# Linear attention and two gated layers on one core: GpSimd's jobs cut up, a new order, another check, and loads on two queues

## The chip, the cores and the metric

One Trainium2 chip, of which one core is used. The core has TensorE (matmuls, PE in the profile), VectorE (DVE), ScalarE (ACT), GpSimd (POOL), and SyncE (SP), which here only issues transfers. The metric is the device time of one execution in microseconds; the median of the runs counts.

## What is computed

A linear attention with decay runs over 4 batches x 8 heads, 768 positions, head width 48. Its result, 3072 tokens of width 384, goes through a gated layer of inner width 1536, then through an RMS norm and a second such layer.

```python
state = 0                                   # per batch and head, 48 x 48
for t in range(768):
    y[t] = r[t] @ (state + (u * k[t]) v[t]^T)
    state = w * state + k[t] v[t]^T
x = y as (3072, 384)
x = (silu(x @ w_gate) * (x @ w_val)) @ w_out            # first layer
xn = x / sqrt(mean(x * x) + 1e-6) * rms_g
out = (silu(xn @ w_gate2) * (xn @ w_val2)) @ w_out2     # second layer
```

The weights of both layers and the queries, keys and values come in as they lie in HBM; weights are 64-bit floats, which the kernel takes apart by their bits.

## The kernel before

The attention is done in 32 units: a batch, a half of the sequence (384 positions) and two heads. Units 0 to 3 (`Unit`) work in chunks of 128, units 4 to 15 (`FullUnit`) in chunks of 64, and the rest (`SplitUnit`) with every operand split into two 16-bit parts. Four units make one block of 384 tokens; there are eight blocks. A block passes each layer in 12 steps, one for each 128 of the inner width. A step has three parts of nine matmuls on TensorE: `step_g` (the gate, `pg`), `step_v` (the value, `pv`), `step_o` (the output, which sums over the 12 steps in three accumulators `po0` to `po2`, one for 128 tokens each). Between them ScalarE computes the silu (`step_s`, tile `sl`), VectorE the product (`step_m`, `sl` again), ScalarE the upper part `hh` (`step_hh`), and GpSimd the lower part `hl` (`step_hl`); `step_o` needs both parts.

The blocks run in the order `ORD`: three blocks of the first layer, then the layers by turns. After a first-layer block its accumulators are copied out (`evacuate`), squared and summed (`squares`, ScalarE), the inverse root and its relatives are formed on three columns (`inverse_rms`, GpSimd: four `ms`, the power `ri`, then `rr` and `iratio`), the tokens scaled, turned and stored. Later they come back (`load_x2`), and `ratio_x2` on GpSimd multiplies them for the second layer's value path.

Each weight tile (one for a step and layer, 24 in all) is decoded: ScalarE takes two passes over it for the check of its range (`w_abs`, `w_check`), VectorE three integer steps (`w_bits`) and one for the lower part (`w_lo`), ScalarE one for the upper (`w_hi`).

The order on every engine is laid out when the program is built. `Plan.add` takes a job with its engine, an expected duration, the jobs it comes after, and a latency; `Plan.run` ranks each job by the longest expected path behind it and fills the engines in expected time, the highest rank first. What a job issues stays together in its engine's queue, and each queue runs in order. A job `D` issues transfers on SP.

The first units: `load` brings keys (`kts`) and queries (`rts`) in four transfers each, all on SP, keys and queries by turns; the values come by GpSimd's own queue. `turn` (VectorE) turns them, `decay_keys` and `grow` (GpSimd, VectorE for the first keys) multiply with the tables G and F, `products` (GpSimd) forms `kr`; `states` (VectorE) carries the state over the chunks, `hand_on` and `states2` (ScalarE) write the carry for the next half and the scaled states for the matmuls. `split_tables` (GpSimd) prepares tables that the units from the fifth on need.

At the end a flag is formed: `check_range` brings all bounds together, `check_last` adds the last block, whose sums of squares come from ScalarE's pass over the accumulators `po`. If the flag is set, a general path runs instead; with these inputs it is not.

Of the kernel before, what the change touches and what calls it, by code (L numbers as in the profile page):

```python
# [18 lines left out]
P = 128  # L19
# [120 lines left out]
def fast_path(ctx, tc, r, k, v, w, u, wg1, wv1, wo1, wg2, wv2, wo2, rms_g, out):  # L140
# [56 lines left out]

    iratio = c_tile([P, NBLK * NG], "iratio")
# [135 lines left out]
    class Unit:  # L334
# [18 lines left out]
        def load(self, which):  # L353
            self.load_rows((self.kts, self.rts)[which], (k, r)[which])
# [127 lines left out]
    class SplitUnit(Unit):  # L482
# [237 lines left out]
    def split_tables():  # L720
# [14 lines left out]
        g.tensor_scalar(out=w_carry, in0=p2[:, 1], scalar1=2.0**AB, scalar2=None, op0=ALU.mult)  # L735
# [128 lines left out]
    def on_act(layer, blk):  # L864

        return () if (layer, blk) == (1, NBLK - 1) else (1,) if layer else (0, 1)
# [15 lines left out]
    def squares(layer, blk):  # L882
        for g in range(NG):
            sq = ev.tile([P, DM], F32, tag="sq", name="sq")
            col = (layer * NBLK + blk) * NG + g
            if (layer, blk) == (1, NBLK - 1):
                nc.scalar.activation(out=sq, in_=acc[layer, blk][g], func=AF.Square, accum_out=ssall[:, col : col + 1],
                                     scale=iratio[:, blk * NG + g : blk * NG + g + 1])
            else:
                nc.scalar.activation(out=sq, in_=post["xo", layer, blk][:, g], func=AF.Square, accum_out=ssall[:, col : col + 1])  # L890

    def inverse_rms(blk):

        g, ms = nc.gpsimd, ev.tile([P, 4, NG], F32, tag="ms", name="ms")
        ss = ssall[:, blk * NG : (blk + 1) * NG]
        for i in range(4):
            g.tensor_scalar(out=ms[:, i], in0=ss, scalar1=1.0 / DM, scalar2=1e-30 if i % 2 else 1e-6, op0=ALU.mult, op1=ALU.add)
        pw_ = post["ri"] = ev.tile([P, 4, NG], F32, tag="ri", name="ri")
        g.tensor_tensor(out=pw_, in0=ms, in1=powers, op=ALU.pow)
# [39 lines left out]
    def ratio_x2(xt, rrow):  # L939
# [84 lines left out]

    def check_last():
# [53 lines left out]
    add("rmsg", "D", 0.5, [("lr", HP - 1)], setup_loads2)  # L1079
    add("bonus", "D", 0.95, [("lr", HP - 1)], setup_loads3)  # L1080
# [4 lines left out]
    add("ws0", "G", 0.4, ["c1"], lambda: nc.gpsimd.memset(wscan, 0.0))  # L1085
# [393 lines left out]
```

## Time and profile before

| | |
|---|---|
| median of 3 runs | 1028.3 us (1027.5 to 1030.15) |
| profiled execution | 1029.09 us, span 1027.4 us |
| mean granted clock | 0.976 |
| TensorE busy | 980.6 us (95%) |
| VectorE, ScalarE, GpSimd busy | 523.4, 519.5, 436.8 us |
| ScalarE in the last four of 40 slices, tenths | 2, 3, 2, 2 |
| one part of a step (nine matmuls) at full clock | 1.46 us |

The profile cuts the span into 40 slices of 25.7 us and gives each engine's busy share in tenths. A clock of 1.00 is TensorE's upper level, 2.4 GHz; 0.50 is its lower level, 1.2 GHz; a mean between them says how a stretch was divided. In lists of instructions a bracket gives the idle time of the engine ahead of the instruction, and who ended it.

### The profile page before, as it was taken

How to read it: one execution, taken by the hardware profiler on the slowest of the kernel's cores; microseconds unless marked ns; L12 is line 12 of the kernel's file. 1: busy time of each engine (PE TensorE's matmuls, PEld its weight loads, DVE VectorE, ACT ScalarE, POOL GpSimd, SP SyncE). 2: the span in 40 equal slices, each digit the busy share in tenths (PEclk: the TensorE clock that was granted, in tenths of full speed). 3: DMA queues.
4: the chain of work that ended last, by engine and by line, in shares of the span. 5: the costliest groups of instructions: out<-in, count | busy, mean ns of one | idle time of the engine just before them, and what ended most of it. 6: DMA issues, size and time to landing. Idle time of an engine off the chain costs nothing.

```text
span 1027.4 us, 19923 instructions
## 1 busy us (share of the span) xinstructions
PE 980.6 (95%) x7903; PEld 612.8 (60%) x7903; DVE 523.4 (51%) x817; ACT 519.5 (51%) x1121; POOL 436.8 (43%) x489
## 2 busy tenths in 40 slices
PE   6887898989999999999999999999999999999996
PEld 3655665646666666666666666666666666666663
DVE  6889997997634434474443534464332412131211
ACT  1987755865644745474455635465453524342322
POOL 9255474444353435544455335544343223321121
PEclk7889998999999999999999999999999999999998
DMA  7988765647441312331122311321010100200000
GB/s 179 226 217 208 219 185 121 169 125 125 108 47 35 84 41 46 58 94 42 33 34 51 83 41 41 64 60 41 2 24 2 54 1 3 53 24 1 24 1 27
DMA packets 152741, 76.87 MB, mean 75 GB/s; under 512 B 115648, under 2 KB 141248, under 8 KB 152640
## 3 DMA queue, kind: packets, MB, share of 16 engines
q1 hardware_dynamic: 152256, 74.93, 30.7%
q8 instruction: 64, 1.05, 0.5%
q0 software_dynamic: 384, 0.59, 0.3%
q14 instruction: 37, 0.30, 0.1%
HBM read 66.03 MB, written 9.45 MB: 73 GB/s over the span
## 4 chain that ended last, share of the span: by engine, by line
PE 70%; DVE 7%; POOL 6%; ACT 6%; issue 4%; DMA 4%; SPq 2%; DVEq 0%; POOLq 0%; ACTq 0%
PE pv L852 22%; PE pg L852 22%; PE po L862 22%; PE py L566 3%; ACT sb L630 2%; POOL hl L992 2%; POOL ap L524 2%; DMA raw<-in_moe_w_out_dram 1%; PE pd L577 1%; DVE st L614 1%; SPq L361 1%; DVE fi L819 1%; DVE fi L821 1%; ACT hh L988 1%; DVE w L842 1%
## 5 line engine op out<-in xcount | busy, mean ns | idle before, releaser
L852 PEld LDWEIGHTS <-w 128*128 128x128 f16 x3456 | 336.4, 99 | 237.4 <-issue 22.3
L992 POOL TENSOR_TENSOR hl<-sl,hh 128x384 f16<-128x384 f32 x191 | 188.2, 986 | 472.4 <-ACT hh L988 465.9
L862 PE MATMUL po<-w,hh 128*128 128x384 f16 x1152 | 282.8, 328 | 1.3 <-ACT xo L878 1.3
L988 ACT ACTIVATE hh<-sl 128x384 f16<-128x384 f32 x192 | 100.0, 521 | 339.9 <-DVE sl L982 194.8
L862 PE MATMUL po<-w,hl 128*128 128x384 f16 x576 | 189.0, 328 | 7.8 <-POOL hl L992 7.7
L982 DVE SCALAR_TENSOR_TENSOR sl<-sl,pv 128x384 f32<-128x384 f32 x96 | 53.1, 554 | 236.0 <-PE pv L852 203.0
L852 PE MATMUL pg<-xh,w 128*128 128x384 f16 x576 | 159.0, 331 | 12.1 <-DVE sl L984 9.6
L852 PE MATMUL pv<-xh,w 128*128 128x384 f16 x576 | 159.4, 332 | 0.0
L862 PEld LDWEIGHTS <-hh 128*128 128x128 f16 x1152 | 111.9, 98 | 74.4 <-issue 2.5
L852 PE MATMUL pv<-x2v,w 128*128 128x384 f16 x864 | 156.2, 326 | 0.0
L852 PE MATMUL pg<-x2g,w 128*128 128x384 f16 x864 | 156.1, 326 | 0.0
L984 DVE TENSOR_TENSOR sl<-sl,pv 128x384 f32<-128x384 f32 x96 | 52.7, 550 | 121.4 <-PE pv L852 117.3
L974 ACT ACTIVATE sl<-pg 128x384 f32<-128x384 f32 x192 | 93.3, 486 | 28.9 <-PE pg L852 27.9
L852 PE MATMUL pg<-xl,w 128*128 128x384 f16 x288 | 95.4, 331 | 1.3 <-DVE xl L479 1.3
L852 PE MATMUL pv<-xl,w 128*128 128x384 f16 x288 | 95.6, 332 | 0.0
L862 PEld LDWEIGHTS <-hl 128*128 128x128 f16 x576 | 56.6, 98 | 47.4 <-POOL hl L992 9.6
L614 DVE TENSOR_TENSOR_SCAN st<-wscan,pd 128x288 f32<-128x288 f32 x28 | 21.0, 750 | 45.6 <-ACT pd L609 26.1
L566 PE MATMUL py<-rp,sb 128*128 128x64 f16 (+1 forms) x400 | 39.3, 212 | 0.4 <-ACT sb L688 0.4
L842 DVE SCALAR_TENSOR_TENSOR w<-fi,w 128x1152 f16<-128x1152 f32 (+1 forms) x30 | 36.6, 1229 | 1.3 <-ACT w L838 1.3
L838 ACT ACTIVATE w<-fi 128x1152 f16<-128x1152 f32 (+1 forms) x30 | 28.8, 963 | 13.0 <-DVE fi L821 12.9
L475 ACT ACTIVATE xh<-py 96x384 f16<-96x384 f32 (+1 forms) x42 | 20.2, 482 | 27.9 <-PE py L566 27.6
L819 DVE SCALAR_TENSOR_TENSOR fi<-raw,fi 128x1152 int32<-128x1152 int32 x21 | 32.4, 1544 | 0.4
(209 smaller groups left out, 1190.2 us busy)
## 6 DMA issues: line engine op xcount, KB each, us to landing
raw<-in_moe_w_out_dram SPq DMA_DIRECT2D x21, 384.0 KB, 5.4
kts<-in_k_dram SPq DMA_DIRECT2D x112, 70.0 KB, 2.8
rts<-in_r_dram SPq DMA_DIRECT2D x112, 70.0 KB, 2.0
xs_d<-tt SPq DMA_DIRECT2D x32, 144.0 KB, 3.8
xt<-xs_d SPq DMA_DIRECT2D x32, 144.0 KB, 3.1
nk<-in_k_dram SPq DMA_DIRECT2D x56, 72.0 KB, 2.7
nr<-in_r_dram SPq DMA_DIRECT2D x56, 72.0 KB, 2.5
out_dram<-xo SPq DMA_DIRECT2D x7, 576.0 KB, 2.9
```

The source lines that it names most:

```text
L566: nc.tensor.matmul(out, a, x, start=i == 0, stop=i == len(pairs) - 1)
L614: nc.vector.tensor_tensor_scan(st, wscan, self.pd, 0.0, ALU.mult, ALU.add)
L819: vec.scalar_tensor_tensor(out=fis[q], in0=high, scalar=-0x40000000, in1=fis[q], op0=ALU.bitwise_and, op1=ALU.bitwise_or)
L838: nc.scalar.activation(out=w_parts(q)[0], in_=fis[q].bitcast(F32), func=AF.Copy, scale=2.0**WS)
L842: nc.vector.scalar_tensor_tensor(out=lo, in0=fis.pop(q).bitcast(F32), scalar=2.0**WS, in1=hi, op0=ALU.mult, op1=ALU.subtract)
L852: nc.tensor.matmul(pt, a[:, kt, :], x[:, kt, :], start=i == 0, stop=i == last)
L862: nc.tensor.matmul(po[g], a[:, sl], x, start=f == 0 and i == 0, stop=f == NF - 1 and i == 2)
L974: nc.scalar.activation(out=sl, in_=job[t]["g"], func=AF.Silu, scale=2.0 ** -(WS + (X2S if J[0] else X1S)))
L982: nc.vector.scalar_tensor_tensor(out=sl, in0=sl, scalar=2.0 ** (H2S - WS - V2S), in1=job[t]["v"], op0=ALU.mult, op1=ALU.mult)
L984: nc.vector.tensor_mul(sl, sl, job[t]["v"])
L988: nc.scalar.activation(out=job[t]["h"][0], in_=job[t]["sl"], func=AF.Copy)
L992: (nc.vector if t == 2 * NT - 1 else nc.gpsimd).tensor_sub(hl, job[t]["sl"], hh)
```

## The change

It has four parts.

- GpSimd: `inverse_rms` becomes three jobs, `ratio_x2` three (one for each third of the width), and the two multiplications of the attention's `products` two.
- The order: most durations and some latencies given to `Plan.add` are others; `split_tables` is placed behind the products of the fourth unit; the transfers of `rmsg` and `u` come behind the last first keys.
- ScalarE's `hand_on` and `states2` of units 0 to 3 go to VectorE, as does the table `w_carry`. The queries of those units are loaded by ScalarE's queue.
- The last block: each step's `hh` is squared and summed on ScalarE (`step_q`), `check_most` and `check_last` look at those sums, and there is no pass over the accumulators; the second of the three accumulators is copied out by ScalarE instead of VectorE.

```diff
+    hsum = c_tile([P, NF], "hsum")
...
-        def load_rows(self, t, src):
+        def load_rows(self, t, src, eng=nc.sync):
...
-                    nc.sync.dma_start(out=t[q : q + 32, 0:RUN],
-                                      in_=bass.AP(src.tensor, self.off(j) + 16 * h, [[NP2 * D, 32], [1, RUN]]))
+                    eng.dma_start(out=t[q : q + 32, 0:RUN],
+                                  in_=bass.AP(src.tensor, self.off(j) + 16 * h, [[NP2 * D, 32], [1, RUN]]))
...
         def hand_on(self):
 
-            nc.scalar.activation(out=carry[self.hp], in_=self.st[:, NC], func=AF.Copy, scale=w_carry[:, self.hp : self.hp + 1])
+            nc.vector.tensor_scalar(out=carry[self.hp], in0=self.st[:, NC], scalar1=w_carry[:, self.hp : self.hp + 1], scalar2=None,
+                                    op0=ALU.mult)
 
         def states2(self):
             for j in range(2):
                 q = slice(64 * j, 64 * j + 64)
-                nc.scalar.activation(out=sbd[self.par][q, :, D * j : D * j + D], in_=self.st[q, 0:NC], func=AF.Copy,
-                                     scale=w128(self.hp)[q])
+                nc.vector.tensor_scalar(out=sbd[self.par][q, :, D * j : D * j + D], in0=self.st[q, 0:NC], scalar1=w128(self.hp)[q],
+                                        scalar2=None, op0=ALU.mult)
...
         def products(self):
-            rk = self.rk = b_tile([P, N2, D], "rk")
-            nc.gpsimd.tensor_mul(rk, self.nr, self.nk)
+            self.rk = b_tile([P, N2, D], "rk")
+            nc.gpsimd.tensor_mul(self.rk, self.nr, self.nk)
+
+        def products2(self):
+            rk = self.rk
             nc.gpsimd.tensor_mul(rk, rk, u2[:, self.hp].unsqueeze(1).to_broadcast([P, N2, D]))
...
-        return () if (layer, blk) == (1, NBLK - 1) else (1,) if layer else (0, 1)
+        return (1,) if layer else (0, 1)
...
+    def inverse_rms2():
+        post["ri"] = ev.tile([P, 4, NG], F32, tag="ri", name="ri")
+        nc.gpsimd.tensor_tensor(out=post["ri"], in0=post.pop("ms"), in1=powers, op=ALU.pow)
...
-        xv = xi.tile([P, KT, TB], F32, tag="tt", name="xv")
-        nc.gpsimd.tensor_mul(xv, xt, rrow.unsqueeze(1).to_broadcast([P, KT, TB]))
-        return xv
+    def ratio_x2(j, kt):
+        xt, rrow = post["xt", j]
+        if not kt:
+            post["xv", j] = xi.tile([P, KT, TB], F32, tag="tt", name="xv")
+        nc.gpsimd.tensor_mul(post["xv", j][:, kt], xt[:, kt], rrow)
...
+    def step_q(t):
+
+        jk = ev.tile([P, TB], BF16, tag="sq", name="jq")
+        f = t - 2 * NT + NF
+        nc.scalar.activation(out=jk, in_=job[t]["h"][0], func=AF.Square, accum_out=hsum[:, f : f + 1])
...
-        ok = ev.tile([P, NG], F32, tag="ok3", name="ok3")
-        nc.vector.tensor_scalar(out=ok, in0=ssall[:, -NG:], scalar1=FINITE, scalar2=None, op0=ALU.is_le)
+        ok = ev.tile([P, 1], F32, tag="ok4", name="ok4")
+        nc.vector.tensor_scalar(out=ok, in0=hsum[:, NF - 1 :], scalar1=FINITE, scalar2=None, op0=ALU.is_le)
...
-    add("rmsg", "D", 0.5, [("lr", HP - 1)], setup_loads2)
-    add("bonus", "D", 0.95, [("lr", HP - 1)], setup_loads3)
+    add("rmsg", "D", 0.5, [("lk", HP - 1)], setup_loads2)
+    add("bonus", "D", 0.95, [("lk", HP - 1)], setup_loads3)
...
-        add(("lk", n), "D", 1.8, [("lr", i - 1)] if i else ["wu"], lambda un=un: (un.stage(un.n), un.load(0)))
-        add(("lr", n), "D", 1.8, [("lk", n)], lambda un=un: un.load(1))
+        add(("lk", n), "D", 1.8, [("at", n)] + ([("lk", i - 1)] if i else ["wu"]), lambda un=un: un.load(0, nc.sync))
+        add(("lr", n), "A", 1.8, [("at", n)] + ([("lr", i - 1)] if i else ["table"]), lambda un=un: un.load(1, nc.scalar), lat=4.0)
...
-        add(("cy", n), "A", 0.25, [("st", n), "tables2"], lambda un=un: un.hand_on())
-        add(("sbd", n), "A", 0.82, [("st", n), "c1"] + prior("y", 2), lambda un=un: un.states2())
+        add(("cy", n), "V", 0.13, [("st", n), "w_carry"], lambda un=un: un.hand_on())
+        add(("sbd", n), "V", 0.4, [("st", n), "c1"] + prior("y", 2), lambda un=un: un.states2())
...
-    add("tables2", "G", 4.5, ["tables", "c1"], split_tables)
+    add("w_carry", "V", 0.1, ["tables"], carry_scale)
+    add("tables2", "G", 4.5, ["tables", "c1", ("rk", HP - 1)], split_tables)
...
-        job_("rk", "G", 1.9, [("nk", n), ("nr", n), "u2", "split"] + p("sums"), lambda un=un: un.products())
-        job_("sums", "V", 0.44, [("rk", n)] + p("eg"), lambda un=un: un.sums())
+        job_("rk", "G", 1.05, [("nk", n), ("nr", n), "split"] + p("sums"), lambda un=un: un.products())
+        job_("rku", "G", 1.05, [("rk", n), "u2"], lambda un=un: un.products2())
+        job_("sums", "V", 0.44, [("rku", n)] + p("eg"), lambda un=un: un.sums())
...
-        add(("abs",) + q, "A", 0.19 + 0.96 * scale, [("w",) + q] + step("chk", prev) + (held(q) if q[0] else []), lambda: w_abs(q))
-        add(("chk",) + q, "A", 0.28 + 0.96 * scale, [("abs",) + q, "c1"], lambda: w_check(q))
+        add(("w",) + q, "D", wcost, ready, (lambda: w_load(*q)) if len(q) == 2 else (lambda: w_load2(q[1], q[2])), lat=5.0 if q[0] else 8.0)
+        add(("abs",) + q, "A", 0.24 + 1.2 * scale, [("w",) + q] + step("chk", prev) + (held(q) if q[0] else []), lambda: w_abs(q))
+        add(("chk",) + q, "A", 0.24 + 1.2 * scale, [("abs",) + q, "c1"], lambda: w_check(q))
...
-            add(("ri", blk), "G", 2.5, [("sq",) + J] + back("put") + back("sc"), lambda blk=blk: inverse_rms(blk))
-            add(("sc", blk), "A", 1.6, [("ri", blk)], lambda blk=blk: normalize(blk))
+            add(("ms", blk), "G", 1.5, [("sq",) + J] + back("ri"), lambda blk=blk: inverse_rms(blk))
+            add(("ri", blk), "G", 2.4, [("ms", blk)] + back("sc") + back("rr"), lambda: inverse_rms2())
+            add(("rr", blk), "G", 1.1, [("ri", blk)] + back("put"), lambda blk=blk: inverse_rms3(blk))
+            add(("sc", blk), "A", 1.75, [("ri", blk)], lambda blk=blk: normalize(blk))
...
-    add("bad", "V", 0.5, ["check", ("sq",) + ORD[-1]] + [("e",) + ORD[-1] + (g,) for g in range(NG)],
+    add("most", "V", 0.4, ["check", ("hq", 2 * NT - 2)], check_most)
+    add("bad", "V", 0.5, ["most", ("hq", 2 * NT - 1), ("o", 2 * NT - 1)] + [("e",) + ORD[-1] + (0,)],
         lambda: post.__setitem__("bad", check_last()))
```

## Rows read from the trace of the kernel before

**Rows 1.** The page's slices: TensorE's busy share in tenths, 40 slices.

```profile
PE   6887898989999999999999999999999999999996
```

**Rows 2.** Stretches: length, busy us of each engine, clock, DMA share, GB/s; last, the first 300 us.

```profile
10.00:20.00 10.00, 3.27 (x18) 3.04 (x18) 9.50 (x19) 0.00 (x0) 9.53 (x27) 0.64 0.72 174
20.00:30.00 10.00, 9.41 (x70) 7.20 (x70) 4.44 (x14) 6.37 (x19) 6.01 (x7) 0.67 0.99 240
...
sum 300.00, PE 264.57 PEld 171.93 DVE 247.67 ACT 193.64 POOL 158.17; mean PE 8.82 PEld 5.73 DVE 8.26 ACT 6.45 POOL 5.27
```

**Rows 3.** Stretches around and behind the long waits, same columns (PE, PEld, DVE, ACT, POOL).

```profile
156.00:163.00 7.00, 5.87 (x28) 2.88 (x30) 2.12 (x5) 4.03 (x7) 4.83 (x8) 0.52 0.63 95
...
150.00:230.00 80.00, 72.39 (x576) 45.15 (x574) 73.04 (x89) 56.21 (x106) 39.36 (x42) 0.94 0.54 138
230.00:300.00 70.00, 70.00 (x548) 45.09 (x546) 44.62 (x77) 38.44 (x93) 31.82 (x37) 0.99 0.54 99
```

**Rows 4.** Waits of TensorE over the whole span: us in total, times, longest.

```profile
PE pg L852 <- DVE sl L984: 9.6, 6, 3.8
PE att L420 <- POOL first L388: 7.8, 1, 7.8
PE po L862 <- POOL hl L992: 7.7, 4, 3.6
```

**Rows 5.** Instructions in order of time at the start: start us, us, engine, line.

```profile
2.25 1.72 SPq L361 DMA_DIRECT2D first<-in_k_dram  x4
...
9.38 1.52 DVE L377 STREAM_TRANSPOSE first<-first 128x384 f32<-128x384 f32 x2
...
10.19 0.31 POOL L725 TENSOR_SCALAR xs<-E 128x32 f32<-128x32 f32 x1
...
10.95 0.38 DVE L306 TENSOR_TENSOR F<-E,pw 128x128 f32<-128x128 f32 x1
...
15.68 1.00 POOL L388 TENSOR_TENSOR first<-first,F 128x384 f32<-128x384 f32 x1
...
17.64 0.42 SPq L770 DMA_DIRECT2D raw<-in_moe_w_gate_dram  x1
...
26.07 0.76 DVE L817 TENSOR_SCALAR fi<-raw 128x1152 int32<-128x1152 int32 x1 [1.99 <-DMA raw<-in_moe_w_out_dram]
```

**Rows 6.** Instructions in order of time behind the first blocks' last steps.

```profile
149.23 0.51 ACT L988 ACTIVATE hh<-sl 128x384 f16<-128x384 f32 x1
149.41 2.90 POOL L897 TENSOR_SCALAR ms<-ssall 128x3 f32<-128x3 f32 x4 [1.51 <-ACT sq L890]
...
152.40 2.92 POOL L899 TENSOR_TENSOR ri<-ms,powers 128x12 f32<-128x12 f32 x1
...
156.16 1.79 POOL L992 TENSOR_TENSOR hl<-sl,hh 128x384 f16<-128x384 f32 x2
...
157.13 0.50 PE L862 MATMUL po<-w,hl 128*128 128x384 f16 x1 [3.56 <-POOL hl L992]
...
228.57 0.50 PE L862 MATMUL po<-w,hl 128*128 128x384 f16 x1 [2.32 <-POOL hl L992]
```

**Rows 7.** Instructions in order of time: a step of the last block.

```profile
985.02 0.91 POOL L992 TENSOR_TENSOR hl<-sl,hh 128x384 f16<-128x384 f32 x1 [3.47 <-ACT hh L988]
...
989.64 0.33 PE L862 MATMUL po<-w,hl 128*128 128x384 f16 x1
```

**Rows 8.** Groups by line and shape: busy us, mean ns of one; idle time ahead.

```profile
L451 ACT ACTIVATE sbd<-st,p 64x144 f32<-64x144 f32 x8 | 3.2, 405 | 0.1
...
L302 DVE TENSOR_SCALAR iE<-iE,zm 128x64 f32<-128x64 f32 x1 | 0.3, 253 | 0.1
```

**Rows 9.** Instructions in order of time at the end.

```profile
1016.68 0.62 DVE L880 TENSOR_SCALAR xo<-po,iratio 128x384 f32<-128x384 f32 x1 [0.43 <-PE po L862]
...
1018.74 1.32 DVE L880 TENSOR_SCALAR xo<-po,iratio 128x384 f32<-128x384 f32 x2 [1.45 <-ACT sq L887]
...
1020.52 0.15 DVE L1033 TENSOR_SCALAR bad<-pc 1x1 int32<-1x1 f32 x1 [0.38 <-PE pc L1031]
```

More of the change, by code (lines that the diff above doesn't have):

```diff
@@ L351, in stage, with load @@
             self.turned = [t[:, n + i * TB : n + (i + 1) * TB].rearrange("p (c t) -> p c t", c=NC) for i in range(2)]
[L353 to L356 removed]
+        def load(self, which, eng):
+            self.load_rows((self.kts, self.rts)[which], (k, r)[which], eng)
+        def load_rows(self, t, src, eng=nc.sync):
             for j in range(2):
@@ L734, in split_tables, with carry_scale @@
             g.tensor_copy(m2[q], mask[q, q])
-        g.tensor_scalar(out=w_carry, in0=p2[:, 1], scalar1=2.0**AB, scalar2=None, op0=ALU.mult)
+    def carry_scale():
+        nc.vector.tensor_scalar(out=w_carry, in0=p2[:, 1], scalar1=2.0**AB, scalar2=None, op0=ALU.mult)
     def split_decay():
@@ L885, in squares @@
             col = (layer * NBLK + blk) * NG + g
[L886 to L890, printed above, removed]
+            nc.scalar.activation(out=sq, in_=post["xo", layer, blk][:, g], func=AF.Square, accum_out=ssall[:, col : col + 1])
     def inverse_rms(blk):
         g, ms = nc.gpsimd, ev.tile([P, 4, NG], F32, tag="ms", name="ms")
+        post["ms"] = ms
         ss = ssall[:, blk * NG : (blk + 1) * NG]
@@ L1023, in check_range, with check_most @@
         nc.vector.tensor_mul(post["m2"], m1[:, 0:1], m1[:, 1:2])
+    def check_most():
+        ok, m1 = ev.tile([P, NF - 1], F32, tag="ok3", name="ok3"), ev.tile([P, 1], F32, tag="m3", name="m3")
+        nc.vector.tensor_scalar(out=ok, in0=hsum[:, : NF - 1], scalar1=FINITE, scalar2=None, op0=ALU.is_le)
+        nc.vector.tensor_reduce(out=m1, in_=ok, axis=AX.X, op=ALU.min)
+        nc.vector.tensor_mul(post["m2"], post["m2"], m1)
     def check_last():
-        ok = ev.tile([P, NG], F32, tag="ok3", name="ok3")
-        nc.vector.tensor_scalar(out=ok, in0=ssall[:, -NG:], scalar1=FINITE, scalar2=None, op0=ALU.is_le)
+        ok = ev.tile([P, 1], F32, tag="ok4", name="ok4")
+        nc.vector.tensor_scalar(out=ok, in0=hsum[:, NF - 1 :], scalar1=FINITE, scalar2=None, op0=ALU.is_le)
         pc = ps.tile([P, 1], F32, tag="att0", name="pc")
-        for i in range(NG + 1):
-            nc.tensor.matmul(pc[0:1], ok[:, i - 1 : i] if i else post["m2"], ones, start=i == 0, stop=i == NG)
+        for i, x in enumerate((post["m2"], ok)):
+            nc.tensor.matmul(pc[0:1], x, ones, start=i == 0, stop=i == 1)
         bad = ev.tile([1, 1], I32, tag="bad", name="bad")
-        nc.vector.tensor_scalar(out=bad, in0=pc[0:1], scalar1=(NG + 1) * P - 0.5, scalar2=None, op0=ALU.is_lt)
+        nc.vector.tensor_scalar(out=bad, in0=pc[0:1], scalar1=2 * P - 0.5, scalar2=None, op0=ALU.is_lt)
         return bad
@@ L1179, in fast_path @@
         for w_, users in (("k", ("rk", "ex", "sq")), ("r", ("rk", "sq")), ("v", ("v1", "sq"))):
-            job_("n" + w_, "D", 0.9, [("lk", n)] + [x for us in users for x in p(us, 2)] + ([("y", NU2 - 1)] if w_ == "v" and n < NU2 + 2 else []),
+            job_("n" + w_, "D", 1.3, [("lk", n)] + [x for us in users for x in p(us, 2)] + ([("y", NU2 - 1)] if w_ == "v" and n < NU2 + 2 else []),
                  lambda un=un, w_=w_: un.load_natural(w_))
@@ L1250, in fast_path @@
         if len(q) == 3:
-            w_jobs(q, 1 / 3, 1.4, [("lo",) + seq[i - 2]], ahead)
+            w_jobs(q, 1 / 3, 2.0, [("lo",) + seq[i - 2]], ahead)
             continue
-        ready = [("lr", HP - 1)] + ([("w", 0, NF - 1)] if q[0] else [])
+        ready = [("lk", HP - 1)] + ([("w", 0, NF - 1)] if q[0] else [])
         tag = RAW_AT[q[0]][q[1]]
@@ L1258, in fast_path @@
             ready += [("y", int(tag[1]))]
-        w_jobs(q, 1.0, 4.1, ready, ahead)
+        w_jobs(q, 1.0, 5.0 if not q[0] else 4.0, ready, ahead)
     for j in range(NBLK):
@@ L1267, in fast_path @@
         turned = [("put", b) for l, b in ORD[: i - 1] if not l][-1:]
-        add(("xv", j), "G", 2.6, [("lx", j)] + turned + ([("vl2", j - 1)] if j else []),
-            lambda j=j: post.__setitem__(("xv", j), ratio_x2(*post["xt", j])))
+        for kt in range(KT):
+            add(("xv", j, kt) if kt < KT - 1 else ("xv", j), "G", 0.9, [("lx", j)] + turned + ([("vl2", j - 1)] if j else [])
+                + ([("xv", j, kt - 1)] if kt else []), lambda j=j, kt=kt: ratio_x2(j, kt))
         free = (last("gv", (1, j - 1)) if j < NBLK - 2 else ["attended"]) + [("lo", 0, NF - 1), ("lo", 0, NF - 2)] * (j == 0)
```

55 lines of the change are left out of this document (29 added, 26 removed).

## The prediction

> **What bounds the kernel now.** I read the slices first, then the stretches, then TensorE's waits, and only then the instructions in the places these named. In the slices TensorE's row [rows 1] is to be read as three parts: digits of 6 to 9 up to the ninth, then unbroken nines, then a last slice at 6. A slice is 25.7 us, so from about 230 us to 1017 TensorE is simply full, and there no other engine's time counts. What can be won lies ahead of 230 us and in the last ten. The sum of the first 300 us gives 264.6 us of TensorE work, that is 35.4 us without any [rows 2]; of the whole span's 46.8 us of idleness nearly all the rest is the end.
>
> In the same stretch VectorE is the second full engine: 73.0 of 80 us between 150 and 230, but only 44.6 of 70 after that [rows 3]. So up to 230 it is TensorE and VectorE by turns, with little room in either, and past it VectorE has 25 us to spare. That is why a late piece of weight decoding can be pushed past 230 and a late piece of a step cannot.
>
> TensorE's waits name three causes worth an edit [rows 4]: for VectorE's product `sl` 9.6 us in six waits, for GpSimd's `first` 7.8 us in one, for GpSimd's `hl` 7.7 us in four. Each longer wait is paid twice. After the 3.56 us wait of 157 us [rows 6] the stretch 156 to 163 shows a granted clock of 0.52, which is mostly the lower level, 1.2 GHz [rows 3]; TensorE was busy 5.87 us in it, and half of that is lost, 2.8 us. I carry that ratio (0.8 us of clock for 1 us of wait) to the others, as an estimate.
>
> **The start: loads on two queues, tables later.** SP issues four descriptors of one key load in 1.72 us [rows 5]; with eight loads of keys and queries that fills SP until the first weight load at 17.64. The change takes four of the eight away: 4 x 1.72 = 6.9 us less on SP, so the first weights are asked for near 10.7. ScalarE pays those 6.9 us while it has nothing else to do: between 10 and 20 it ran no instruction [rows 2]. The weights landed for VectorE at 26.07 [rows 5], and between 20 and 30 VectorE worked 4.4 of 10 us [rows 2], so it has the room to take them earlier.
>
> The other half is GpSimd. Queries were turned by 10.90 and table F was there at 11.33, but GpSimd began `split_tables` at 10.19 and came to the first `grow` at 15.68 [rows 5]. With that job behind the products of the fourth unit, `grow` starts near 11.4: 4.3 us earlier, and TensorE, which waited 7.8 us for it [rows 4], with it. The 5.5 us of `split_tables` don't vanish; they are hidden in GpSimd's idleness between the fourth products and the split units. Should that cover fail, the fifth unit is late.
>
> Both halves give the same shift of what follows, not twice. The floor is nothing (the saved time runs into another queue), the ceiling the 6.9 us; I take the GpSimd row's 4.3 us, since it is a measured wait on the path. DMA share was 0.72 in 10 to 20 and 0.99 in 20 to 30 [rows 2], so some of the early issue can only fill the first hole. The Trainium skill (DMA: Bandwidth & Descriptors, Issuing engines are not separate DMA queues) says that issuing from several engines saves the sequencer's issue time and nothing else, as all run on the same 16 engines. By it the 0.99 stays a ceiling; were the weights bound by it alone, the sum would lose the whole 4.3 us.
>
> **Carry and first states on VectorE.** Twelve instructions leave ScalarE, eight of 405 ns and four shorter [rows 8], some 4.6 us, and come to VectorE. The trace has none of that shape there. A tensor_scalar of 128x64 took 253 ns; ScalarE's time for the shape is the upper bound. Twelve times that is 3.0 to 4.9 us; I take 3.0, the form being the same engine's. VectorE's 5.6 us of idleness between 20 and 30 [rows 2] hide it if it falls there; if not, 3 us come on the path. Against it stands one change of engine less between `st` and the next unit's `st`, and a freer ScalarE before the first step's `x_hi`. I put the pair at nothing, with -2 and +3 as ends.
>
> The Trainium skill (SBUF — State Buffer, Who interferes with whom) speaks against this move: a tensor_scalar in a two-port mode takes the port pair that VectorE and GpSimd share for its whole length, and GpSimd blocks. The trace has such pairs: four `ms` and one `ri` took 2.90 and 2.92 us beside a busy VectorE [rows 6]. By the rule the moved work could hold GpSimd up by its own 3.0 us, and the sum would be 3 us smaller.
>
> **GpSimd's pieces.** `inverse_rms` was one job, planned at 2.5 us. In block 0 `hh` was ready at 149.74, yet `hl` ran only at 156.16, behind ms (2.90), ri (2.92) and three small ones; TensorE stood 3.56 us [rows 6]. In block 1 it stood 2.32 us for the same reason. With three jobs the product can come between. What is then late next? `ri` is still one instruction, 2.9 us at worst. In the full part `hl` begins at 985.02, ends 0.91 later, and is used at 989.64: 3.7 us to spare [rows 7]. So one piece fits into the slack, and the whole job of 6.7 us didn't. Gone would be 3.56 + 2.8 and 2.32 + 1.9 (by the ratio) = 10.6 us. The later blocks show no such wait, so nothing there. Bounds: nothing, and 10.6. As VectorE is nearly full between 150 and 230 [rows 3] I take two thirds, 7.1 us: the rest will be met by a late `sl`. The products `rk` were two instructions and stay two. `ratio_x2` becomes three instructions for one, a little more GpSimd time, all past 230 and beside a full TensorE: nothing.
>
> **The order by measured durations.** This moves everything between 20 and 230 us, and the trace can't show where. The 9.6 us of waits for `sl` [rows 4] are what it can win, 17 us with the clock by the ratio; three more waits of the longest kind (3.8 us) are what it can cost, 20 us. The planner was wrong mostly about GpSimd and loads, which is priced above already. I take nothing, and keep both ends for the range.
>
> **The end.** After the last `po`, VectorE copies group 0 from 1016.68; then it stands until 1018.74, because ScalarE's squares of the same accumulators come in between; the flag follows at 1020.52 and ends at 1020.67 [rows 9]. Now the twelve squares run on ScalarE beside the steps, where the page's last full slices have it at 2 to 3 tenths, group 1 goes by ScalarE, and groups 0 and 2 by VectorE. Group 2 is whole two thirds of a nine-matmul part (1.46 us) later than group 0, near 1017.6; a copy of 0.66 us (half of the row's 1.32), the check of 0.2, the two products and the flag of 0.6 us end near 1018.9: 1.8 us less. Below it could be 1.0 (the last square, behind `hh`, holds the check), above 2.4 (flag ahead of group 2). The 6.7 us from there to the span's end stay, and the last store, issued right after its copy, goes with them.
>
> **The sum** against the profiled execution's 1029.1 us (span 1027.4): -4.3 - 7.1 - 1.8 = -13.2, so 1015.9. The median of the runs is 1028.3, 0.8 lower; I say 1015.
>
> **Rivals.**
> VectorE takes over (A): with every wait for GpSimd gone the steps wait for `sl` instead, since 73.0 of 80 us are taken [rows 3]. Then the end's 1.8 and a third of the other 11.4 remain: -5.6, 1022.7. Against it: 25 free us right behind 230. 0.20.
>
> The order also heals the `sl` waits (B): half of 17 us more and the whole 10.6: -4.3 - 10.6 - 1.8 - 8.6 = -25.3, 1003. For it: the costs it is laid out by are those that the rows show. Against: VectorE's share leaves little room. 0.13.
>
> The change does not reach the path (C): order and start cancel, the `hl` waits move to another step, and the end's 1.8 is left: 1026.5. 0.08.
>
> Slower (D): VectorE's queue is in order, and `sums` stands in it waiting for the second product, which is now a job of its own that other GpSimd work may be laid ahead of; `sl` stands behind `sums`, and TensorE behind `sl`. Each such wait costs 3.8 + 3.0 = 6.8 us. One of them eats the start and the end (6.1), so it decides from the second on, with the `hl` gain lost to it: +7.5, 1036. For it: six waits on `sl` exist already, and two parts of a job can be torn apart. Against: the planner now knows what each part costs. 0.13.
>
> **Numbers.** The forecast (1009 to 1020) has 0.46. This kernel's measurement can tell 0.3%, 3.1 us. Faster by more: the forecast, A and B, 0.79; within: C, 0.08; slower: D, 0.13. The range 1002 to 1029 leaves out most of D and the far half of B.
>
> **What would show it.** First `grow` near 11.4 and first `att` near 12.5 (right start); first weights asked for near 10.7; an `hl` between `ms` and `ri` of blocks 0 and 1, and no TensorE wait over 1 us there; in the last block no squares of `po`, and the flag 1.3 us behind the last `po`. The prediction is wrong if TensorE's idleness in the first 300 us is not below 28 us, or if new waits of 3 us or more for `sl` appear between 40 and 150.

## The result, and the profile after

| | before | after |
|---|---|---|
| median of 4 runs | 1028.35 us (1027.5 to 1030.15) | 1016.56 us (1014.21 to 1017.55) |
| profiled execution, span | 1029.09, 1027.4 us | 1014.21, 1012.4 us |
| TensorE busy, idle in the span | 980.6, 46.8 us | 971.8, 40.6 us |

The ratio is 0.988, with a 95% interval of 0.9857 to 0.9903: 12 us faster, where 13 were forecast. The profiled execution of after is the fastest of its runs, so the two traces differ by 15.0 us and the medians by 11.8.

The page of the kernel after: engines' busy time, then the slices of TensorE and of its granted clock, which answer to [rows 1].

```profile
PE 971.8 (96%) x7899; PEld 607.9 (60%) x7899; DVE 534.0 (53%) x832; ACT 518.8 (51%) x1128; POOL 448.4 (44%) x504
...
PE   7678899999999999999999999999999999999996
...
PEclk8989999999999999999999999999999999999998
```

From the sixth slice to the last but one there are only nines now. First reading: the 15.0 us fall into 6.2 us less idleness (46.8 to 40.6) and 8.8 us less busy time for almost the same matmuls (7903 records before, 7899 after). A higher clock is enough for the second part: between 10 and 300 us the records show the lower level, 1.2 GHz, for 41.0 us before and for 20.5 us after, and half of this difference is 10 us. The stretches of after answer to [rows 2, 3]. Behind the length stand the busy us of TensorE, its weight loads, VectorE, ScalarE and GpSimd, each with its number of instructions, then clock, DMA share and GB/s:

```profile
10.00:20.00 10.00, 6.87 (x40) 4.82 (x41) 9.33 (x24) 2.36 (x7) 7.33 (x10) 0.67 0.88 216
20.00:30.00 10.00, 10.00 (x106) 9.51 (x104) 9.20 (x20) 8.50 (x20) 7.18 (x11) 0.99 1.08 246
...
0.00:300.00 300.00, 269.16 (x2154) 175.04 (x2155) 257.73 (x374) 191.70 (x375) 168.13 (x187) 0.97 0.70 165
...
150.00:230.00 80.00, 77.76 (x646) 50.03 (x642) 75.32 (x93) 58.30 (x109) 48.28 (x45) 1.00 0.72 170
```

Between 150 and 230 TensorE's idleness fell from 7.6 us [rows 3] to 2.2 and the clock went from 0.94 to 1.00. The first 300 us still hold 30.8 us of idleness (35.4 before [rows 2]). VectorE, 75.3 of 80 us, is fuller than it was.

TensorE's waits after (line, what ended them, total, times, longest), which answer to [rows 4]:

```profile
PE pg L860 <- DVE sl L995: 12.1, 7, 5.0
PE att L422 <- POOL first L390: 3.3, 1, 3.3
PE pg L860 <- DVE w L850: 3.2, 1, 3.2
PE po L870 <- POOL hl L1003: 3.1, 2, 1.8
PE pg L860 <- DVE xl L482: 2.6, 1, 2.6
```

`hl` went from 7.7 to 3.1 and `first` from 7.8 to 3.3. `sl` grew from 9.6 to 12.1, all of it between 40 and 130 us, and the wait for VectorE's decoding (`w`) is new. The one for its splitting (`xl`) doubled; before, it was:

```profile
PE pg L852 <- DVE xl L479: 1.3, 1, 1.3
```

The start after, in order of time, against [rows 5]:

```profile
2.25 9.49 SPq L363 DMA_DIRECT2D first<-in_k_dram  x12
2.82 12.07 ACTq L363 DMA_DIRECT2D first<-in_r_dram  x14
...
11.26 1.23 POOL L390 TENSOR_TENSOR first<-first,F 128x384 f32<-128x384 f32 x1 [1.17 <-DVE F L308]
12.54 1.51 PE L422 MATMUL att<-first 64*128 64x128 f32 x12 [3.31 <-POOL first L390]
14.97 0.35 SPq L778 DMA_DIRECT2D raw<-in_moe_w_gate_dram  x1
...
38.55 0.32 PE L860 MATMUL pg<-xh,w 128*128 128x384 f16 x1 [0.58 <-ACT xh L478]
41.45 0.48 PE L860 MATMUL pg<-xl,w 128*128 128x384 f16 x1 [2.58 <-DVE xl L482]
49.23 0.50 PE L860 MATMUL pg<-xh,w 128*128 128x384 f16 x2 [3.22 <-DVE w L850]
57.05 0.48 PE L860 MATMUL pg<-xh,w 128*128 128x384 f16 x1 [5.04 <-DVE sl L995]
```

`grow` and `att` come when the prediction said. The first step on the weights comes early too, 7.8 us ahead of the same row of before:

```profile
46.37 0.32 PE L852 MATMUL pg<-xh,w 128*128 128x384 f16 x1 [2.47 <-ACT xh L475]
```

The first weights' loads, asked for at 14.97, are later than the 10.7 forecast: sharing the list saved SP 2.7 us and not 6.9. With two queues SP spent 0.79 us on a descriptor (9.49 / 12) where it spent 0.43 [rows 5], and ScalarE 0.86, but such a row counts the gaps between its issues. A single issue of these loads took 0.31 to 0.43 us in both traces. The gaps are SP's waits for earlier transfers to land, first after, then before:

```profile
SPq L363 <- DMA first<-in_k_dram: 6.5, 9, 1.6
...
SPq L361 <- DMA first<-in_r_dram: 0.7, 2, 0.6
SPq L361 <- DMA first<-in_k_dram: 0.4, 2, 0.2
```

Before, an issue waited for the transfer eight ahead of it (the one at 9.80 for that of 5.87, which landed at 9.78). After, it waited for the one four ahead on its own queue (ScalarE's at 12.47 for that of 7.99, which landed at 12.46).

Behind block 0, against [rows 6]:

```profile
149.12 0.52 ACT L999 ACTIVATE hh<-sl 128x384 f16<-128x384 f32 x1 [4.44 <-DVE sl L995]
149.29 2.00 POOL L902 TENSOR_SCALAR ms<-ssall 128x3 f32<-128x3 f32 x4
151.38 0.92 POOL L1003 TENSOR_TENSOR hl<-sl,hh 128x384 f16<-128x384 f32 x1
...
154.36 2.31 POOL L906 TENSOR_TENSOR ri<-ms,powers 128x12 f32<-128x12 f32 x1
```

`hl` stands between `ms` and `ri`, and no wait of TensorE follows. Behind block 1 it comes out otherwise: `hl` runs only behind four slow `ms`, and TensorE still waits 1.83 us, where it waited 2.32. No lower clock follows it (1.00 from 200 to 262):

```profile
209.95 3.96 POOL L902 TENSOR_SCALAR ms<-ssall 128x3 f32<-128x3 f32 x4 [1.54 <-ACT sq L894]
...
214.96 0.34 PE L870 MATMUL po<-w,hl 128*128 128x384 f16 x1 [1.83 <-POOL hl L1003]
```

Where along the kernel the time came from is read by the start of each step's `hh`, after less before: +2.3 us at step 0, -4.9 at 11, -3.6 at 14, -10.1 at 16, -10.6 at 20, -15.2 at 30, -12.7 at 36, -13.6 at the last step; the end makes it -15.0. The big drop, 6.5 us between steps 14 and 16, lies where the first long `hl` wait was. The -15.2 at step 30 is a peak that falls back: the next step has -10.5, and step 25, ahead of the `hl` waits behind block 1, already had -12.6. So no gain behind block 1 can be read from it.

The end, against [rows 9]:

```profile
1003.59 0.58 ACT L886 ACTIVATE xo<-po,iratio 128x384 f32<-128x384 f32 x1 [0.86 <-PE po L870]
1003.71 0.33 PE L870 MATMUL po<-w,hl 128*128 128x384 f16 x1
...
1004.08 0.62 DVE L888 TENSOR_SCALAR xo<-po,iratio 128x384 f32<-128x384 f32 x1 [0.36 <-PE po L870]
...
1005.04 0.15 DVE L1057 TENSOR_SCALAR bad<-pc 1x1 int32<-1x1 f32 x1 [0.28 <-PE pc L1055]
```

The flag ends 1.14 us behind the last `po` (3.05 before), and the span 8.39 us behind it (9.79 before): of the flag's 1.91 us the span keeps 1.40.

### The profile page after: what moved, and what is told of

It reads as the page before. It is cut to its first block, busy times and chain, and to the rows that moved or that the text cites. A ratio compares the mean times of both kernels' runs of the same rounds, so it can differ in the third digit from the quotient of the medians.

```text
span 1012.4 us, 19953 instructions
## 1 busy us (share of the span) xinstructions
PE 971.8 (96%) x7899; PEld 607.9 (60%) x7899; DVE 534.0 (53%) x832; ACT 518.8 (51%) x1128; POOL 448.4 (44%) x504
## 4 chain that ended last, share of the span: by engine, by line
PE 70%; DMA 10%; DVE 8%; POOL 4%; SPq 3%; ACT 3%; issue 2%; DVEq 0%; POOLq 0%; ACTq 0%
PE pv L860 22%; PE po L870 22%; PE pg L860 22%; DMA raw<-in_moe_w_out_dram 3%; PE py L572 3%; DMA raw<-in_moe_w_val_dram 2%; DMA xs_d<-tt 1%; ACT sb L636 1%; PE pd L583 1%; DMA raw<-in_moe_w_gate_dram 1%; DMA first<-in_k_dram 1%; POOL ap L527 1%; DVE fi L829 1%; DVE fi L827 1%; DVE st L620 1%
## 5 line engine op out<-in xcount | busy, mean ns | idle before, releaser
L860 PE MATMUL pg<-xh,w 128*128 128x384 f16 x576 | 158.9, 331 | 15.9 <-DVE sl L995 12.1
L860 PE MATMUL pv<-xh,w 128*128 128x384 f16 x576 | 156.9, 327 | 0.0
L531 POOL TENSOR_TENSOR rk<-nr,nk 128x288 f32<-128x288 f32 x28 | 31.3, 1118 | 1.9 <-DVE gd L539 1.4
```

Source lines behind the costliest of these rows:

```text
L531: nc.gpsimd.tensor_mul(self.rk, self.nr, self.nk)
L860: nc.tensor.matmul(pt, a[:, kt, :], x[:, kt, :], start=i == 0, stop=i == last)
```

## Experiments

Each was measured beside runs of the kernel before, whose medians stayed between 1027.6 and 1028.9 us. Ratios are to those; the kernel after has 0.988.

**The end alone** (on the kernel before).

```diff
+        if J == ORD[-1]:
+            add(("hq", t), "A", 0.7, [("hh", t)] + (prev("hq", 1) if f else []), lambda t=t: step_q(t))
...
-    add("bad", "V", 0.5, ["check", ("sq",) + ORD[-1]] + [("e",) + ORD[-1] + (g,) for g in range(NG)],
+    add("most", "V", 0.4, ["check", ("hq", 2 * NT - 2)], check_most)
+    add("bad", "V", 0.5, ["most", ("hq", 2 * NT - 1), ("o", 2 * NT - 1)] + [("e",) + ORD[-1] + (0,)],
```

> The kernel before, with the last block's check and the copy of its second accumulator as in the changed kernel, nothing else. Theory (the parts add up): the flag ends 1.3 us behind the last po instead of 3.1, the time is 1.4 to 1.8 us below the kernel before (ratio 0.9985), and TensorE's idleness in the first 300 us stays at 35 us. Rival (the flag is not what ends the span): no difference. Rival (any change re-lays the whole order): the first 300 us differ by more than 2 us too.

Measured 1027.87 us, 0.9997 [0.9983, 1.0011]. In its trace the flag ends 1.14 us behind the last `po`, as in the kernel after, and the span 7.74 us behind it, 2.04 less than before. The head of the same execution was slower than that of before with the same order there on every engine (first `att` at 16.92, 39.5 us of TensorE's idleness in the first 300 us for 35.4, span 1029.2): two traces of one order can lie 4 us apart there, and small differences between single traces below are to be read with that. So the step is real in the trace and no larger than the scatter of the head in the time.

**`inverse_rms` in one job again, planned honestly** (on the kernel after).

```diff
-            add(("ms", blk), "G", 1.5, [("sq",) + J] + back("ri"), lambda blk=blk: inverse_rms(blk))
-            add(("ri", blk), "G", 2.4, [("ms", blk)] + back("sc") + back("rr"), lambda: inverse_rms2())
-            add(("rr", blk), "G", 1.1, [("ri", blk)] + back("put"), lambda blk=blk: inverse_rms3(blk))
+            add(("ri", blk), "G", 5.0, [("sq",) + J] + back("put") + back("sc"),
+                lambda blk=blk: (inverse_rms(blk), inverse_rms2(), inverse_rms3(blk)))
...
```

> The changed kernel, with inverse_rms as one job again, planned at 5.0 us, the sum of its three pieces' durations. Theory (the pieces remove the hl waits): TensorE's waits for hl behind blocks 0 and 1 come back at 2 to 4 us each, with the lower clock behind them, and the time rises by 5 to 8 us, to about 1023. Rival (an honest duration is enough, since the planner then lays hl ahead of the job): the time stays within 2 us of the changed kernel's 1016.6.

Measured 1016.46 us, 0.9897 [0.9874, 0.992]: no change, as the rival said, but not for its reason. Behind block 0 the whole job still stands ahead of `hl`, which starts 4.9 us after `hh` was ready (150.46), and yet TensorE doesn't wait, because its own order is another. It first does `pa` and `py` of the attention:

```profile
150.12 2.01 POOL L902 TENSOR_SCALAR ms<-ssall 128x3 f32<-128x3 f32 x4
...
154.93 0.55 PE L572 MATMUL py<-ap,nv 128*96 128x64 f32 x4
...
155.36 0.92 POOL L1003 TENSOR_TENSOR hl<-sl,hh 128x384 f16<-128x384 f32 x1
...
156.85 0.49 PE L870 MATMUL po<-w,hh 128*128 128x384 f16 x2
```

The kernel after has `pa` and `py` there as this run has. Before, neither stood there: `po` began at 153.07, and TensorE stood until 157.13 [rows 6].

```profile
153.07 0.50 PE L862 MATMUL po<-w,hh 128*128 128x384 f16 x2
```

What this run leaves of the `hl` waits (the longest behind block 1):

```profile
PE po L870 <- POOL hl L1003: 4.4, 3, 2.0
```

**The same, planned at the old 2.5 us.**

```diff
-            add(("ri", blk), "G", 5.0, [("sq",) + J] + back("put") + back("sc"),
+            add(("ri", blk), "G", 2.5, [("sq",) + J] + back("put") + back("sc"),
```

> The changed kernel with inverse_rms as one job again, planned at 2.5 us as in the kernel before (in the run with one job planned at 5.0 us the time did not change). Theory (either the pieces or an honest duration cures the wait, and neither is needed beside the other): now the waits for hl behind blocks 0 and 1 come back, 2 to 4 us each, and the time rises by 4 us or more. Rival (the wait was an accident of the old layout): no change, within 2 us of 1016.6.

Measured 1021.82 us, 0.9925 [0.9903, 0.9946]: 5 us lost by the medians, though the interval overlaps that of the run ahead. The instructions are those of that run; one number differs. In its trace the long wait is back behind block 1, but not behind block 0, where `py` still comes ahead of `po`:

```profile
221.73 0.50 PE L870 MATMUL po<-w,hl 128*128 128x384 f16 x1 [3.99 <-POOL hl L1003]
```

The stretch behind it (length, then busy us of TensorE, its loads, VectorE, ScalarE, GpSimd, clock, DMA share), against the 0.52 of [rows 3]:

```profile
221.00:228.00 7.00, 6.27 (x36) 3.23 (x36) 1.94 (x4) 3.92 (x10) 2.58 (x3) 0.51 0.65 133
```

So behind block 1 the pieces or a true duration shorten the wait (1.83 and 2.03 us for 3.99). The longer wait of before, behind block 0, needs neither: it went with the order.

**All old durations and latencies** (on the kernel after; the pieces share the old numbers).

```diff
-        job_("nv", "D", 2.0, [("lk", n), ("z", ("vb", "nv")[un.par])] + p("y", 2), lambda un=un: un.load_v())
+        job_("nv", "D", 0.9, [("lk", n), ("z", ("vb", "nv")[un.par])] + p("y", 2), lambda un=un: un.load_v())
...
-            add(("ri", blk), "G", 2.4, [("ms", blk)] + back("sc") + back("rr"), lambda: inverse_rms2())
+            add(("ri", blk), "G", 1.2, [("ms", blk)] + back("sc") + back("rr"), lambda: inverse_rms2())
```

> The changed kernel with the durations and latencies of the kernel before in the planner (pieces share the old duration of their job). Theory (durations are worth nothing by themselves): within 3 us of the changed kernel's 1016.6, and no hl wait over 2 us behind blocks 0 and 1. Rival (the order laid out with measured durations is what the change lives on): 5 us or more slower, with longer waits for sl and hl in the first 230 us.

Measured 1031.18 us, 1.0028 [1.0013, 1.0042]. All the rest of the change together, pieces and second queue among it, without the new numbers is worth nothing. The waits for `sl` are shorter than after, not longer as the rival said; TensorE's longest waits there:

```profile
PE pd L688 <- DMA vb<-in_v_dram: 7.3, 1, 7.3
PE pg L860 <- DVE sl L995: 5.1, 4, 2.6
PE po L870 <- POOL hl L1003: 5.1, 5, 2.4
```

**The new numbers alone** (on the kernel before; `inverse_rms` in one job at 5.0; the second layer's input waits for its gains, as in the kernel after).

```diff
-        job_("nv", "D", 0.9, [("lk", n), ("z", ("vb", "nv")[un.par])] + p("y", 2), lambda un=un: un.load_v())
+        job_("nv", "D", 2.0, [("lk", n), ("z", ("vb", "nv")[un.par])] + p("y", 2), lambda un=un: un.load_v())
...
-            add(("ri", blk), "G", 2.5, [("sq",) + J] + back("put") + back("sc"), lambda blk=blk: inverse_rms(blk))
+            add(("ri", blk), "G", 5.0, [("sq",) + J] + back("put") + back("sc"), lambda blk=blk: inverse_rms(blk))
...
```

> The kernel before with the changed kernel's durations and latencies in the planner (inverse_rms, ratio_x2 and the products stay whole, at the sum of their pieces), and the second layer's input waiting for its gains as in the changed kernel; nothing else. Theory now (the gain is the order by measured durations, and the rest of the change is worth little without it): 8 us or more faster, below 1020, with no wait for hl over 2 us behind blocks 0 and 1. Rival (durations pay only together with the earlier start): within 4 us of the kernel before.

Measured 1020.26 us, 0.992 [0.9901, 0.994]. Two thirds of the gain come with numbers that change no instruction (the added dependency was not run by itself). The `hl` waits of [rows 4] are nearly gone though the job is whole:

```profile
PE po L862 <- POOL hl L992: 1.8, 1, 1.8
```

**Only the transfers' numbers old** (on the kernel after).

```diff
-        add(("w",) + q, "D", wcost, ready, (lambda: w_load(*q)) if len(q) == 2 else (lambda: w_load2(q[1], q[2])), lat=5.0 if q[0] else 8.0)
+        add(("w",) + q, "D", wcost, ready, (lambda: w_load(*q)) if len(q) == 2 else (lambda: w_load2(q[1], q[2])))
...
-        w_jobs(q, 1.0, 5.0 if not q[0] else 4.0, ready, ahead)
+        w_jobs(q, 1.0, 4.1, ready, ahead)
```

with `nv` and the natural loads back at 0.9.

> The changed kernel with only the transfers' numbers of the kernel before in the planner (durations of weight, natural and value loads, latency 4 us for weights instead of 8 and 5). Theory (the planner's picture of the loads is what matters in the first 70 us): most of the 15 us between the changed kernel and the one with all old numbers comes back, 1025 or above, with a wait for a value load near 60 us. Rival (the engines' durations are what matters): within 4 us of 1016.6.

Measured 1028.16 us, 0.9998 [0.9984, 1.0012]: the whole gain is lost. The first `hh` is 9.4 us later than before, and TensorE's longest wait is new. The profile puts it down to `rk`, which `pd` doesn't read; `pd` reads `vb`, whose load SP issued at 58.00, so it may be the late value load that was expected:

```profile
62.67 1.59 PE L688 MATMUL pd<-vb,ef 64*64 64x48 f32 x19 [6.44 <-POOL rk L531]
```

**Only the engines' durations old.**

```diff
-            add(("ri", blk), "G", 2.4, [("ms", blk)] + back("sc") + back("rr"), lambda: inverse_rms2())
+            add(("ri", blk), "G", 1.2, [("ms", blk)] + back("sc") + back("rr"), lambda: inverse_rms2())
...
-        add(("hl", t), "V" if t == 2 * NT - 1 else "G", 1.08, [("hh", t)], lambda t=t: step_hl(t))
+        add(("hl", t), "V" if t == 2 * NT - 1 else "G", 0.95, [("hh", t)], lambda t=t: step_hl(t))
```

> The changed kernel with only the engines' durations of the kernel before (ScalarE, VectorE and GpSimd jobs; pieces share the old duration), the transfers' numbers new. Theory (the transfers' numbers matter): within 4 us of 1016.6. Rival (the engines' durations matter): 1024 or above, with waits for sl and hl of 2 us and more between 80 and 230 us.

Measured 1022.09 us, 0.9941 [0.992, 0.9961]: 5.5 us lost, between what the theory and the rival said, and the `hl` waits are 6.0 us in five.

**Only the weights' latency old.**

```diff
-        add(("w",) + q, "D", wcost, ready, (lambda: w_load(*q)) if len(q) == 2 else (lambda: w_load2(q[1], q[2])), lat=5.0 if q[0] else 8.0)
+        add(("w",) + q, "D", wcost, ready, (lambda: w_load(*q)) if len(q) == 2 else (lambda: w_load2(q[1], q[2])))
```

> The changed kernel with one thing of the transfers' numbers old: the weights' latency in the planner is 4.0 us again instead of 8 (first layer) and 5. Theory (a too short latency puts the decode of weights that have not landed ahead of the attention's jobs in the engines' queues): most of the 11.6 us that all the transfers' numbers were worth comes back, 1023 or above, with hh of the first step 5 us or more later. Rival (the durations of the loads matter, as they set SP's order): within 3 us of 1016.6.

Measured 1017.73 us, 0.9893 [0.9867, 0.9918]: no difference, as the rival said. By exclusion, what counts of the transfers' numbers is the time each load holds SP's place in the plan, not when it is expected to land. Which load's time it is was not run.

**A nudge**: `hl` planned at 0.99 for 1.08, to see what another layout by chance is worth.

```diff
-        add(("hl", t), "V" if t == 2 * NT - 1 else "G", 1.08, [("hh", t)], lambda t=t: step_hl(t))
+        add(("hl", t), "V" if t == 2 * NT - 1 else "G", 0.99, [("hh", t)], lambda t=t: step_hl(t))
```

> The changed kernel with one number of the planner changed: 0.99 instead of 1.08 for hl on GpSimd (the trace's mean is 0.986). It measures what a re-laid order is worth by chance. Theory (the gain lies in the named parts): within 2 us of 1016.6. Rival (the result is a lucky layout): it moves by 4 us or more.

Measured 1015.01 us, 0.9884 [0.9868, 0.99]: the same as after, within 1.6 us. It says little of chance, because it laid out almost the same order: VectorE's is that of after instruction for instruction, and on the other engines a few neighbours change places. Three other runs here laid out other orders (`inverse_rms` in one job at 5.0, the old latency, and `split_tables` below move 153, 61 and 90 of VectorE's 832 instructions) and lie within 1.2 us of after; two more, below, lie 7 us away on either side.

**The first queries on SP again.**

```diff
-        add(("lk", n), "D", 1.8, [("at", n)] + ([("lk", i - 1)] if i else ["wu"]), lambda un=un: un.load(0, nc.sync))
-        add(("lr", n), "A", 1.8, [("at", n)] + ([("lr", i - 1)] if i else ["table"]), lambda un=un: un.load(1, nc.scalar), lat=4.0)
+        add(("lk", n), "D", 1.8, [("at", n)] + ([("lr", i - 1)] if i else ["wu"]), lambda un=un: un.load(0, nc.sync))
+        add(("lr", n), "D", 1.8, [("at", n), ("lk", n)], lambda un=un: un.load(1, nc.sync))
```

> The changed kernel with the first queries on SP's queue again, keys and queries by turns; all else as changed. In the changed kernel the first weights were asked for at 14.97 us, not near 10.7, since a descriptor of the two queues takes 0.78 us there instead of 0.45. Theory (the second queue is worth what it won, 2.7 us of issue): the first weights at 17 to 18 us and a time 1 to 3 us above 1016.6. Rival (it is the second queue that lets everything start): 4.3 us or more, 1021. Rival (the layout heals it): no difference.

Measured 1023.64 us, 0.995 [0.9929, 0.9972]: 7 us lost. SP's queue shows four descriptors in 1.8 us again, and the first weights 2.5 us later than after:

```profile
15.60 1.81 SPq L363 DMA_DIRECT2D first<-in_r_dram  x4
17.46 0.42 SPq L778 DMA_DIRECT2D raw<-in_moe_w_gate_dram  x1
```

The other 4.5 us are not the issue itself: the trace, of an execution 3.5 us over the median, has an `hl` wait of 3.51 us at 227.95 and one of 3.9 us for `rp` that after doesn't have. Whether they come of the one queue or of the order laid out around it is open. The Trainium skill (DMA: Bandwidth & Descriptors, Issuing engines are not separate DMA queues) says that a second issuing engine saves only its sequencer's time. The traces agree: the 16 issues left on SP took it 5.6 us where the 32 of before took 12.9, and most of the 7 us saved went into the 6.5 us of waits for transfers to land.

**`split_tables` free to come first.**

```diff
-    add("tables2", "G", 4.5, ["tables", "c1", ("rk", HP - 1)], split_tables)
+    add("tables2", "G", 4.5, ["tables", "c1"], split_tables)
```

> The changed kernel with split_tables free to come first on GpSimd, as before; all else as changed. Theory (grow's start is a wait on the path): the first att at 15 to 17 us instead of 12.5 and a time 2 to 4 us above 1016.6. Rival (the first 60 us are bound by the weights' arrival and VectorE, so the early att is lost anyway): first att late, time within 1.5 us. Rival (the planner itself puts it behind, as the first grow ranks higher with the new durations): att at 12.5 and no difference.

Measured 1015.99 us, 0.9884 [0.9856, 0.9911]: no difference in the times, which leave room for some 3 us, though `att` waits again and the first step on the weights starts 4.5 us later than after:

```profile
16.63 1.64 PE L422 MATMUL att<-first 64*128 64x128 f32 x9 [8.55 <-POOL first L390]
...
43.03 0.32 PE L860 MATMUL pg<-xh,w 128*128 128x384 f16 x1 [1.65 <-ACT xh L478]
```

So the times give the wait for `first` no price in this layout. What sets the steps' pace there instead isn't shown; VectorE, which decodes the weights, is busy for 18.9 of the 20 us between 30 and 50 in this run and for 19.2 after.

**The carry and first states on ScalarE again.**

```diff
-        add(("cy", n), "V", 0.13, [("st", n), "w_carry"], lambda un=un: un.hand_on())
-        add(("sbd", n), "V", 0.4, [("st", n), "c1"] + prior("y", 2), lambda un=un: un.states2())
+        add(("cy", n), "A", 0.3, [("st", n), "w_carry"], lambda un=un: un.hand_on())
+        add(("sbd", n), "A", 0.82, [("st", n), "c1"] + prior("y", 2), lambda un=un: un.states2())
```

(and the copies themselves by `nc.scalar.activation`)

> The changed kernel with one part undone: the states and the carry of the first four units are copied by ScalarE again, as before. Theory (the sum's own step, 0): within 2 us of the changed kernel's 1016.6, that is 1014.5 to 1018.5, for both engines have idle time to spare around these copies and the early start has shown itself worth nothing. Rival 1 (ScalarE's relief is part of the gain): 1020 or more, with the first step on the weights 2 us or more later than 38.55. Rival 2 (VectorE's added 4 us count, since it is the busiest of the three small engines in the first 40 us): 1013 or less.

Measured 1009.55 us, 0.9817 [0.979, 0.9843]: 7 us faster than after, the fastest of all, and faster than both kernels; this interval and that of after don't meet. The second rival came true; neither 0 nor the end of +3 held it. In the first 50 us VectorE works 39.0 us for 42.3, ScalarE 29.8 for 27.4; TensorE's waits:

```profile
PE pg L859 <- DVE sl L994: 8.9, 7, 4.0
PE att L422 <- POOL first L390: 3.4, 1, 3.4
PE pd L687 <- DMA vb<-in_v_dram: 2.8, 1, 2.8
PE pa L681 <- DVE rp L516: 2.3, 2, 2.0
```

The `hl` waits are gone from the list and `sl` is 3.2 us shorter. The `hh` of the first 25 steps stand within 3 us of after's, sometimes earlier, sometimes later; the gain that stays (3.3 us between the two profiled executions) is made between steps 23 and 37, long after the copies. So VectorE's added work does count, or the order laid out around them is luckier. Which of the two is open; the nudge, which left VectorE's order as it was, can't tell.

## Why the prediction was right, and where it was not

The time was right (1015 for 1016.56, inside the forecast's own 1009 to 1020), but by a sum whose terms belong elsewhere.

**The start, -4.3.** The measured shift of `grow` and `att` came true to 0.2 us, and the times show no price for it (`split_tables` free to come first). The step that failed is "I take the GpSimd row's 4.3 us, since it is a measured wait on the path": a wait of TensorE is on the path only if what follows doesn't wait again. TensorE came to the first step 7.8 us earlier (38.55 for 46.37), and `hh` of that step was 2.3 us later than before, behind waits for `xl`, `w` and `sl`. Undoing the second queue, whose half was not to count twice, costs 7 us in this layout. The mis-sized term is 6.9 us off SP, which measured 2.7: the prediction took SP's time on the list for issuing alone, and with half of the list SP waited 6.5 us for transfers to land.

**Carry and states, 0.** The twelve copies on VectorE after, lines and durations in ns (least, median, longest):

```profile
L448 DVE TENSOR_SCALAR carry<-st,w_carry x4: 233/270/942, 22.6 to 37.3; 128x48 f32<-128x48 f32 x4
...
L454 DVE TENSOR_SCALAR sbd<-st,p x8: 331/356/361, 19.1 to 36.4; 64x144 f32<-64x144 f32 x8
```

By the medians that is 8 x 0.356 + 4 x 0.270 = 3.9 us, and the longest `carry` adds 0.7: inside the 3.0 to 4.9 said, nearer to the upper end. The cover is the likely fault: between 20 and 30 VectorE is at 9.2 of 10 us now, where [rows 2] had 4.4, and at 7.6 without the copies. That idleness was spent twice, on the earlier weights and on these copies. Undone, the kernel gains 7 us; why so much is open. The rule of the Trainium skill weighed there (SBUF — State Buffer, Who interferes with whom), that such work holds GpSimd up, isn't seen: GpSimd was busy 36.1 us of the first 50 without the copies and 35.5 with them, and its products beside the copies took their usual 1.00 us. If anything it went the other way, once: the 942 ns `carry` (22.57 to 23.51) ended with the GpSimd product that had begun ahead of it (22.47 to 23.46).

**GpSimd's pieces, -7.1.** The number was near by luck. Behind block 0 the wait went with its clock, 6.5 us for 6.4; behind block 1, 1.83 of the 2.32 us stayed. No third was lost to a late `sl`: between 150 and 230 TensorE has no wait for `sl` at all. The cause was wrong: "So one piece fits into the slack, and the whole job of 6.7 us didn't" names the slack of before's order. With `pa` and `py` ahead of `po` the whole job fits behind block 0, even planned at 2.5 us; only behind block 1 does that number bring a wait back (3.99 us). By these runs the gain belongs to the order.

**The order, 0.** This step failed most: "The planner was wrong mostly about GpSimd and loads, which is priced above already. I take nothing". Of the loads only SP's list at the start was priced, not what the planner held the later ones for. With the old numbers the kernel is at 1031.2, 15 us above after, and of the two halves the transfers' weigh most (11.6 us, the engines' 5.5). The bounds (-17 to +20) held it. What the undone parts cost doesn't add up: the two halves alone make 17.1 us, with 14.6 for both at once.

**The end, -1.8.** 1.4 in the trace, the mechanism as told; in the time of the end alone it can't be told from nothing. The prediction's own terms, from 1017.6, add up to 1019.1 and not 1018.9, so 1.6.

**Signs.** Of the signs for it, `grow`, `att`, the flag and `hl` of block 0 came; the first weights at 10.7 and block 1 without a wait over 1 us didn't. Of those against it, the idleness came, 30.8 us for 28, and an `sl` wait of 5.04 us at 57; before had two of 3 us and more between 40 and 150 (3.81 at 64.88, 3.00 at 100.89), so this one is new in its place only. The time came right nonetheless: the signs counted waits, not clock. The ratio of 0.8 us of clock for 1 us of wait was 8.8 / 6.2 = 1.4 over the kernel. Rival A did not come as told: `sl` waits grew by 2.5 us, but ahead of 130 us, and where the `hl` waits went, VectorE, at 75.3 of 80 us, held TensorE up for 0.3 us once.

## What to carry to other kernels

Where an order is laid out by expected durations, replace these by the ones of a profile first, the transfers' above all, and judge structural edits only then: 8 of 12 us came with numbers, and the wait that an edit seemed to heal was filled by the new order with other work. Before a wait is counted as gain, follow its engine to its next wait; and don't spend one engine's idleness on two edits. Each part of a change that pays as a whole is worth undoing once: without one of these the kernel was 7 us faster.

## What was not expected of the hardware

An issue of these loads took 0.31 to 0.43 us on one queue and on two, but with two each issue came 0.79 and 0.86 us behind the last, held by transfers that had yet to land: the 32 issues took two queues 13.2 us (1.69 to 14.89) and one 15.4 (2.25 to 17.60). And TensorE's busy time depended on where its waits lie more than on their sum: the run with `inverse_rms` planned at 2.5 us had 41.8 us of idleness and 980.4 of busy time, where after had 40.6 and 971.8.
